# Four transfers instead of five for the last weight matrix of a decode step, and the order of the blocks that use it

## The chip, the cores and the metric

The kernel runs on one core of a Trainium2 chip. Its time is the device time of one execution in microseconds (us). Four executions of the kernel before the change took 84.27 to 84.72 us, with a median of 84.5 us.

## The reference

One decode step of a transformer block with conditioning, for a batch of 4 rows of 512 numbers, in bfloat16. A vector `mod` is computed from the condition `c`; it holds shifts, scales and gates. Then come attention over the last 1024 positions of a cache (32 query heads, 8 key and value heads, 128 numbers a head), and a feed-forward layer:

```python
mod = (silu(c) @ w_mod)                       # sa, ca, ga, sb, cb, gb: 512 each
h = layernorm(x) * (1 + ca) + sa
x = x + ga * attention(h, k_cache, v_cache, wq, wo)
h = layernorm(x) * (1 + cb) + sb
x = x + gb * (relu(h @ w1) @ w2)              # w1 512 x 1792, w2 1792 x 512
```

Some 32 MB of weights and cache are read from memory for 4 rows, so there is little arithmetic for each byte.

## The kernel before

**Transfers.** All large loads are issued by SP on one DMA queue, in the order in which they are needed: `w_mod`, the first two pieces of the key cache, `wq`, the other keys, the values, `wo` in four pieces (lines 120 and 121), `w1` whole (line 126), and `w2` in the pieces that `W2_CHUNKS` lists (lines 128 to 133). A transfer has a semaphore that is counted up when all of it has landed. Eight such semaphores are used in turn, so SP issues a transfer only when the one eight places earlier has landed. `w2` has 1792 rows. They are handled as 14 blocks of 128 rows, and a transfer of `e` blocks puts `e` successive rows of `w2` into each of the 128 partitions, as one run of `e` times 1024 bytes. Within a transfer of `e` blocks, block `m` therefore holds every `e`-th row.

**The feed-forward layer.** The first product must give its results in the same order of rows. So `w1_cols` (line 477) picks 128 columns of `w1` for block `m` with a step of `e` between them. `ffn1` (line 489) computes `relu(h @ w1)` for a range of blocks, transposed: for each block, four weight loads of 128 such columns, one for each quarter of the contraction, with a matmul of 32 columns behind each. Three VectorE operations (lines 498, 500 and 501) then form `uT`. It runs for blocks 0 to 7 and then for blocks 8 to 13.

**The second product.** `closing` (line 192) issues the matmuls of one or more blocks of `w2`. The 512 output columns are cut into four groups of 128. Each block takes two steps `x`, and in each of them two matmuls of 128 columns, `g` = 0 and 1, which use two of TensorE's four groups of 32 array columns side by side. Blocks in `ZUP` (0, 1, 2, 3, 6, 7, 8) add into `za_ps` in column groups 2 and 3; the others (4, 5, 9, 10, 11, 12, 13) add into `z_ps` in column groups 0 and 1. Where `closing` is given one block of each kind, the four matmuls of a step run in all four column groups together; blocks that stand alone use half of the array. TensorE takes its matmuls in the order in which they are written. A block waits for its own transfer and for its part of `uT`.

**The end.** Once block 8, the last of `ZUP`, is added, ScalarE copies `za_ps` to `zc` (line 513), and VectorE multiplies it by the gate and adds the residual (lines 514 and 515). Once block 13 is added, VectorE forms `zg` from `z_ps` (line 520) and adds `zc` to it (line 522). VectorE works in this order, so `zg` stands behind both operations on `zc`. Two small transfers, from SP and from ScalarE's queue, write the result.

The order of the work on TensorE, ScalarE, VectorE and GpSimd is the order in which the program is written.

Of the kernel before, what the change touches and what calls it, by code (L numbers as in the profile page):

```python
# [17 lines left out]
def kernel(  # L18
# [23 lines left out]
    FT = Dff // P  # L42
# [82 lines left out]
    w2_sb = w12[:, DT * Dff:DT * Dff + FT * D].rearrange("p (m n) -> p m n", m=FT)  # L125
    nc.sync.dma_start(out=w1_sb, in_=B_w1.rearrange("(p t) n -> p t n", t=DT))

    W2_CHUNKS = [(0, 4), (4, 4), (8, 3), (11, 2), (13, 1)]
    assert sum(e for _, e in W2_CHUNKS) == FT
    w2_dst = w12[:, DT * Dff:DT * Dff + FT * D]  # L130
    for (m0, e) in W2_CHUNKS:
        nc.sync.dma_start(out=w2_dst[:, m0 * D:(m0 + e) * D],
# [59 lines left out]
    def closing(parts):  # L192
        for x in range(NX):
            for (ps, q, j, src, rhs, start, stop, cols) in parts:
                for g in range(2):
                    q0 = (q + g) * CG
                    nc.tensor.matmul(out=ps[q0:q0 + CG, cols], lhsT=rows(src, j, x), rhs=rhs(2 * x + g),  # L197
                                     start=start and x == 0, stop=stop and x == NX - 1, tile_position=(0, q0))
# [278 lines left out]
    def w1_cols(t, m):  # L477
        m0, e = [ch for ch in W2_CHUNKS if ch[0] <= m][-1]
        return w1_sb[:, t, m0 * P + m - m0:(m0 + e) * P:e]
# [9 lines left out]
    def ffn1(m0, m1):  # L489

        u4_ps = psA.tile([P, m1 - m0, NR, 2, B], f32, tag="t", name=f"u_ps_{m0}")
        u_ps = u4_ps[:, :, 0]
        for m in range(m0, m1):
            for t in range(DT):
                nc.tensor.matmul(out=u4_ps[:, m - m0].rearrange("p n s b -> p n (s b)"), lhsT=w1_cols(t, m),  # L495
                                 rhs=ab[:, t].rearrange("p s b -> p (s b)").unsqueeze(1).to_broadcast([P, NR, 2 * B]), start=(t == 0), stop=(t == DT - 1))
        us = work.tile([P, m1 - m0, B], f32, name=f"us_{m0}")
        nc.vector.tensor_tensor(out=us[:], in0=u_ps[:, :, 0, :], in1=rstd2[:].unsqueeze(1).to_broadcast([P, m1 - m0, B]),
                                op=ALU.mult)
        nc.vector.tensor_tensor(out=us[:], in0=us[:], in1=u_ps[:, :, 1, :], op=ALU.add)  # L500
        nc.vector.tensor_scalar_max(out=put(uT32[:, m0:m1, :]), in0=us[:], scalar1=0.0)  # L501

    def zpart(m):
        mine = ZUP if m in ZUP else ZLOW
        return (za_ps if m in ZUP else z_ps, 2 if m in ZUP else 0, m, uT32, lambda j: w2_sb[:, m, j * DH2:(j + 1) * DH2],
                m == mine[0], m == mine[-1], slice(None))

    for (m0, m1) in [(0, 8), (8, FT)]:
        ffn1(m0, m1)
    for ms in [(0,), (1,), (2, 4), (3, 5), (6,), (7,), (8, 9)]:  # L510
        closing([zpart(m) for m in ms])
    zc = work.tile([2 * CG, DH2], f32, name="zc")
    nc.scalar.copy(out=zc[:], in_=za_ps[2 * CG:P, :])
    nc.vector.tensor_tensor(out=zc[:], in0=zc[:], in1=gb2[:], op=ALU.mult)  # L514
    nc.vector.tensor_tensor(out=zc[:], in0=zc[:], in1=x12_ps[:], op=ALU.add)
    for m in range(10, FT):
        closing([zpart(m)])

    zg = work.tile([2 * CG, DH2], f32, name="zg")
# [36 lines left out]
```

## Time and profile before

| | |
|---|---|
| median of four executions | 84.5 us (84.27 to 84.72) |
| the profiled execution's own time | 84.35 us |
| its span, from the first to the last instruction | 82.6 us |
| mean granted TensorE clock | 0.791 |
| TensorE busy with matmuls, with weight loads | 57.0 us, 46.9 us |
| VectorE, ScalarE, GpSimd busy | 26.5, 23.8, 6.0 us |
| read from memory | 31.99 MB, 387 GB/s over the span |

The span is 1.75 us shorter than the profiled execution's own time; what lies around it is not in the trace. Times within the trace are counted from the start of the span. In a line of the timeline the first number is the start in us and the second how long the group of instructions took, from the start of the first to the end of the last; "x8" is their number; PE is TensorE's matmuls, PEld its weight loads, DVE VectorE, ACT ScalarE and SP the engine that issues the loads. Square brackets hold the idle time of the engine before the group and what ended it. In a table of windows a row holds a stretch of the span, its length, the busy time and number of instructions of PE, PEld, DVE, ACT and POOL, then the granted TensorE clock (1.00 is full), the busy share of the core's 16 DMA engines, and GB/s.

### The profile page before, as it was taken

What the parts mean: (1) busy time and instruction counts of PE and PEld (TensorE: products, weight loads), DVE (VectorE), ACT (ScalarE), POOL (GpSimd) and SP (SyncE); (2) the same over time, 40 slices, a digit from 0 to 9 for tenths busy, and PEclk for the clock granted to TensorE, in tenths of its full rate; (3) what the DMA queues carried; (4) which work ended last, traced back from release to release, by engine and by line L of the source; (5) the groups of instructions that cost most, each with busy time, mean ns of one, the idle gap of its engine ahead of it and who ended that gap; (6) DMA issues with size and microseconds to landing.
All of it is one profiled execution on the core that took longest, in us unless ns stands there. A gap on an engine that the chain in (4) does not pass through costs nothing.

```text
span 82.6 us, 2381 instructions
## 1 busy us (share of the span) xinstructions
PE 57.0 (69%) x1068; PEld 46.9 (57%) x1068; DVE 26.5 (32%) x76; ACT 23.8 (29%) x38; POOL 6.0 (7%) x21
## 2 busy tenths in 40 slices
PE   0001006999962989999999932999837579899950
PEld 0000006995852973997777702999837239577830
DVE  0111300368043010275466576850001320150450
ACT  3201001664302000597779809540100010002010
POOL 5895000000000000000000000000000000000000
PEclk9999999999985555699999999569655555555599
DMA  1999999998979999999999999999999999999700
GB/s 25 325 463 429 393 421 425 571 413 365 492 329 409 441 421 417 429 437 409 421 437 433 417 417 437 417 425 433 433 413 417 437 417 440 432 389 411 304 30 2
DMA packets 4257, 32.14 MB, mean 389 GB/s; under 512 B 528, under 2 KB 664, under 8 KB 1304
## 3 DMA queue, kind: packets, MB, share of 16 engines
q1 hardware_dynamic: 4192, 31.99, 92.6%
q8 instruction: 8, 0.13, 0.6%
q0 software_dynamic: 32, 0.00, 0.0%
q10 hardware_dynamic: 24, 0.01, 0.0%
q14 instruction: 1, 0.01, 0.0%
HBM read 31.99 MB, written 0.00 MB: 387 GB/s over the span
## 4 chain that ended last, share of the span: by engine, by line
DMA 80%; PE 8%; SPq 4%; DVE 3%; issue 1%; ACT 0%; DVEq 0%
DMA k<-in_A_k_cache_dram 33%; DMA v<-in_A_v_cache_dram 24%; DMA wo_sb<-in_A_wo_dram 24%; SPq L86 2%; PE za_ps L197 2%; PE y_ps L440 2%; PE u_ps L495 1%; PE x_ps L197 1%; PE sc_ps L446 1%; SPq L101 1%; PE s_ps L457 1%; SPq L96 0%; SPq L95 0%; DVE zc L514 0%; DVE res L522 0%
## 5 line engine op out<-in xcount | busy, mean ns | idle before, releaser
L228 PE MATMUL ktp<-ident_k,k 128*128 128x128 bf16 x256 | 18.2, 240 | 5.6 <-DMA k<-in_A_k_cache_dram 5.6
L228 PEld LDWEIGHTS <-k 128*128 128x128 bf16 x256 | 17.1, 109 | 8.3 <-DMA k<-in_A_k_cache_dram 5.7
L233 ACT COPY kT<-ktp 128x1024 bf16<-128x1024 bf16 x16 | 15.5, 1015 | 17.4 <-PE ktp L228 16.3
L231 DVE COPY kT<-ktp 128x1024 bf16<-128x1024 bf16 x16 | 11.1, 692 | 16.2 <-PE ktp L228 15.9
L363 PE MATMUL oT_ps<-pT,v 128*128 128x16 bf16 x256 | 7.1, 172 | 1.7 <-issue 1.7
L363 PEld LDWEIGHTS <-v 128*128 128x128 bf16 x256 | 7.0, 100 | 1.7 <-issue 1.7
L240 PE MATMUL sc_ps<-kT,qpad 128*32 128x512 bf16 x64 | 5.6, 445 | 0.4 <-DVE qpad L329 0.4
L380 PE MATMUL pT_ps<-ident_bf,p_rep 128*128 128x128 bf16 x32 | 3.3, 292 | 2.9 <-DVE p_rep L374 2.9
L203 PE MATMUL tp<-ident_bf,cx_sb 8*128 8x8 bf16 x4 | 0.3, 174 | 7.2 <-DMA cx_sb<-in_A_x_dram 7.2
L380 PEld LDWEIGHTS <-p_rep 128*128 128x128 bf16 x32 | 2.9, 135 | 3.4 <-DVE p_rep L374 3.4
L325 PE MATMUL qT_ps<-hT,wq_sb 128*128 128x4 bf16 x128 | 3.6, 166 | 1.4 <-DVE ab L318 1.4
L325 PEld LDWEIGHTS <-wq_sb 128*128 128x128 bf16 x128 | 3.5, 104 | 1.5 <-DMA wq_sb<-in_A_wq_dram 1.5
L203 PEld LDWEIGHTS <-cx_sb 8*128 8x128 bf16 x4 | 0.2, 114 | 7.2 <-DMA cx_sb<-in_A_x_dram 7.2
L432 ACT COPY y<-y_ps 128x256 f32<-128x256 f32 x1 | 0.4, 373 | 9.0 <-DVE y L431 9.0
L440 PEld LDWEIGHTS <-wo_sb 128*128 128x128 bf16 x64 | 2.5, 121 | 0.4 <-DMA wo_sb<-in_A_wo_dram 0.4
L374 DVE TENSOR_TENSOR p_rep<-e_sb,mi 128x512 int32<-128x512 int32 x4 | 2.5, 688 | 0.7 <-ACT e_sb L369 0.7
L440 PE MATMUL y_ps<-o,wo_sb 128*128 128x32 bf16 x64 | 2.5, 193 | 0.3 <-DMA wo_sb<-in_A_wo_dram 0.3
L405 DVE TENSOR_TENSOR oT_sb<-oT_ps,rb 128x128 bf16<-128x128 f32 x1 | 0.3, 291 | 7.5 <-PE oT_ps L363 7.5
L436 PEld LDWEIGHTS y_ps<-sel_b,y 128*128 128x128 f32 x8 | 1.8, 329 | 1.4 <-DVE y L431 1.4
L427 PE MATMUL y_ps<-wo_sb,o 128*32 128x512 bf16 x16 | 1.9, 619 | 0.9 <-DVE o L418 0.9
L240 PEld LDWEIGHTS <-qpad 128*32 128x32 bf16 x64 | 1.3, 103 | 2.2 <-DVE qpad L329 0.7
L197 PEld LDWEIGHTS <-uT 128*32 128x32 bf16 x56 | 2.1, 127 | 0.7 <-DVE uT L501 0.3
(115 smaller groups left out, 57.7 us busy)
## 6 DMA issues: line engine op xcount, KB each, us to landing
k<-in_A_k_cache_dram SPq DMA_DIRECT2D x8, 1024.0 KB, 28.1
v<-in_A_v_cache_dram SPq DMA_DIRECT2D x8, 1024.0 KB, 19.6
wq_sb<-in_A_wq_dram SPq DMA_DIRECT2D x1, 4096.0 KB, 23.5
wo_sb<-in_A_wo_dram SPq DMA_DIRECT2D x4, 1024.0 KB, 19.6
wmod_sb<-in_w_mod_dram SPq DMA_DIRECT2D x1, 2304.0 KB, 9.4
w<-in_B_w_dram SPq DMA_DIRECT2D x1, 1792.0 KB
w<-in_B_w_dram SPq DMA_DIRECT2D x2, 512.0 KB, 19.6
wmod_sb<-in_w_mod_dram SPq DMA_DIRECT2D x1, 768.0 KB, 4.4
```

The lines of the kernel that those rows point to most:

```text
L197: nc.tensor.matmul(out=ps[q0:q0 + CG, cols], lhsT=rows(src, j, x), rhs=rhs(2 * x + g), start=start and x == 0, stop=stop and x == NX - 1, ...
L228: nc.tensor.transpose(out=tp[:, ii, :], in_=k_tiles[gi][:, iq * IQ + ii, :], identity=ident_k)
L231: nc.vector.tensor_copy(out=dst, in_=tp[:])
L233: nc.scalar.copy(out=dst, in_=tp[:])
L240: nc.tensor.matmul(out=sc_ps[hw * CG:(hw + 1) * CG, half * HALF:(half + 1) * HALF], lhsT=qpad[:, b, par, hw, :], rhs=kT[:, half * (NI // 2 ...
L325: nc.tensor.matmul(out=qT_v[:, hq, :], lhsT=wq_sb[:, t, hq * Dh:(hq + 1) * Dh], rhs=hT[:, t, :], start=(t == 0 and hq == 0), stop=(t == DT ...
L363: nc.tensor.matmul(out=oT_ps[:, hw, par].rearrange("p b r -> p (b r)"), lhsT=v_tiles[h][:, i, :], rhs=pT[:, i, c0:c0 + B * rep], start=(fi ...
L374: nc.vector.tensor_tensor(out=p_w[:, ws, :], in0=e_w[:, ws].unsqueeze(2).to_broadcast([P, WQ // 2, B]), in1=mi4[:].unsqueeze(1).to_broadca ...
L380: nc.tensor.transpose(out=tp[:, ii, :], in_=p_rep[:, i // 2, :, i % 2], identity=ident_bf[:])
L427: nc.tensor.matmul(out=y4_ps[q0:q0 + CG, :], lhsT=o4[:, l, g % 2, g // 2, :], rhs=wo_sb[:, g, l, :], start=(g == 0 and l < 4), stop=(g == ...
L436: nc.tensor.matmul(out=y32_ps[:, t, :], lhsT=y4[:, t, :], rhs=sel_b[:], start=(t == 0), stop=False)
L440: nc.tensor.matmul(out=y32_ps[:, m, :], lhsT=wo_sb[:, g, l, m::DT], rhs=o4[:, l, g % 2, g // 2, :], start=False, stop=(g == NP - 1 and l = ...
```

## The change

`w2` is cut into transfers of 6, 5, 2 and 1 blocks in place of 4, 4, 3, 2 and 1. The step between the columns of `w1` follows it through `w1_cols`. In the second product, block 7 is issued together with block 9 and block 8 together with block 10, where block 7 stood alone, blocks 8 and 9 were together and block 10 came alone after the operations on `zc` had been written.

```diff
-    W2_CHUNKS = [(0, 4), (4, 4), (8, 3), (11, 2), (13, 1)]
+    W2_CHUNKS = [(0, 6), (6, 5), (11, 2), (13, 1)]
...
-    for ms in [(0,), (1,), (2, 4), (3, 5), (6,), (7,), (8, 9)]:
+    for ms in [(0,), (1,), (2, 4), (3, 5), (6,), (7, 9), (8, 10)]:
         closing([zpart(m) for m in ms])
     zc = work.tile([2 * CG, DH2], f32, name="zc")
     nc.scalar.copy(out=zc[:], in_=za_ps[2 * CG:P, :])
     nc.vector.tensor_tensor(out=zc[:], in0=zc[:], in1=gb2[:], op=ALU.mult)
     nc.vector.tensor_tensor(out=zc[:], in0=zc[:], in1=x12_ps[:], op=ALU.add)
-    for m in range(10, FT):
+    for m in range(11, FT):
         closing([zpart(m)])
```

## The prediction

> **What bounds the kernel now.** I read the page's slices first, then the chain that ended last, then the issues of the transfers, and then the last six microseconds instruction by instruction, since the change touches nothing earlier. The page's row of DMA shares:
>
> ```profile
> DMA  1999999998979999999999999999999999999700
> ```
>
> The 16 DMA engines are full from the second slice to the thirty-seventh: the kernel is a stream of loads with work hung on it. The chain of waits says the same, and what follows the stream (start, us, what):
>
> ```profile
> 51.13 19.47 DMA wo_sb<-in_A_wo_dram
> ...
> 78.05 0.59 PE za_ps L197 x9
> ...
> 78.78 0.27 ACT zc L513
> ...
> 79.08 0.30 DVE zc L514
> ...
> 79.39 0.28 DVE zc L515
> 79.67 0.26 DVE zg L520
> ```
>
> So the end of the span hangs on the last blocks of `w2`, by way of `za_ps`, its copy and three VectorE operations. When the blocks arrive follows from the issues (w is `w1` and `w2`; KB each, us from issue to landing):
>
> ```profile
> w<-in_B_w_dram SPq DMA_DIRECT2D x2, 512.0 KB, 19.6
> w<-in_B_w_dram SPq DMA_DIRECT2D x1, 384.0 KB, 17.4
> w<-in_B_w_dram SPq DMA_DIRECT2D x1, 256.0 KB, 15.7
> w<-in_B_w_dram SPq DMA_DIRECT2D x1, 128.0 KB, 13.5
> ```
>
> and from SP's timeline, whose last load is this one:
>
> ```profile
> 65.76 0.33 SPq L132 DMA_DIRECT2D w<-in_B_w_dram  x1
> ```
>
> The last transfer lands at 65.76 + 13.5 = 79.26; in the same way (issues at 55.99, 58.43, 60.86 and 63.29; the view of the tile w gives 20.2 for the first, so 19.0 for the second) the others land at 76.19, 77.43, 78.3 and 78.95. TensorE's timeline over the end:
>
> ```profile
> 74.90 1.14 PEld L495 LDWEIGHTS <-w 128*128 128x128 bf16 x32 [0.57 <-DMA w<-in_B_w_dram]
> 75.86 0.83 PEld L495 LDWEIGHTS <-w 128*128 128x128 bf16 x27
> 76.96 0.29 PE L197 MATMUL za_ps<-w,uT 128*32 128x128 bf16 x2 [0.16 <-DVE uT L501]
> 77.78 0.64 PE L197 MATMUL za_ps<-w,uT 128*32 128x128 bf16 x8
> 78.34 0.29 PE L197 MATMUL za_ps<-w,uT 128*32 128x128 bf16 x2
> 78.98 0.62 PE L197 MATMUL z_ps<-w,uT 128*32 128x128 bf16 x12
> ```
>
> The reader sees `ffn1` start when `w1` lands, the second product start at 76.96 when `uT` is made, blocks 6 and 7 (the x8) at 77.78, and then two starts, 78.34 for block 8 and 78.98 for block 11, each just after a landing. The clock over this stretch, from the table of windows:
>
> ```profile
> 77.50:78.75 1.25, 1.25 (x38) 1.16 (x35) 0.00 (x0) 0.00 (x0) 0.00 (x0) 0.50 0.49 185
> 78.75:79.00 0.25, 0.22 (x7) 0.06 (x3) 0.00 (x0) 0.22 (x1) 0.00 (x0) 0.85 0.17 57
> 79.00:79.25 0.25, 0.25 (x8) 0.25 (x8) 0.17 (x1) 0.04 (x1) 0.00 (x0) 1.00 0.00 0
> ```
>
> It goes from half to full at about 78.82 (0.85 is 0.3 of the slice at 0.5 and 0.7 at 1.0). Only half of the DMA engines still work after 77.5: the others are done.
>
> **The change, step by step.**
>
> *One transfer fewer.* The bytes are the same. A straight line through 1.24 us for 4 blocks (76.19 to 77.43), 0.90 for 3 and 0.64 for 2 (TensorE's releases 77.44, 78.34, 78.98) gives 0.30 us a block and 0.03 a transfer, with 0 and 0.12 as the ends that its pairs allow. I take 0.03. The first new transfer (blocks 0 to 5) lands near 76.8, before `uT` needs it. The second (6 to 10) ends where the old third ended, with one transfer fewer ahead of it: block 6 is released at 78.34 - 0.03 = 78.31. Blocks 11 and 12 come at 78.95 and block 13's transfer lands at 79.23. SP issues four times in place of five, 0.33 us each, beside a queue that is full for some 13 us ahead: nothing. No other queue is passed by anything, and the output's transfers only take other semaphores, whose earlier transfers (`wo`) are long landed.
>
> *Blocks 6 and 7 lose their early transfer.* This is the main term. They ran from 77.78, on the second old transfer; now block 6 waits at the head of TensorE's queue until 78.31, and behind it wait 7 to 10, all of the tail, and `zc`. From the release to the end of `za_ps`, the old order had two steps (8 with 9, x = 0 and 1): 78.34 to 78.75 (the copy starts at 78.78, 0.03 after). The new one has six: two of block 6, two of 7 with 9, two of 8 with 10. A step costs 0.107 us: four take 0.64 in the x8 row, of which the last matmul is 0.31. The first interval after a stall is 0.08 to 0.09 (0.40 less that 0.31). So the sixth step starts at 78.31 + 0.08 + 4 x 0.107 = 78.82, just as the clock rises; the last matmul takes 0.22 at full clock (the shortest of `z_ps`, 216 ns), and `za_ps` ends at 79.04 in place of 78.75. The copy moves from 78.78 to 79.07: 0.29 later. Blocks 9 and 10 ride beside and cost no step.
>
> *What the tail gives back.* Block 10 leaves the tail, which holds 11 to 13 alone: they end at about 79.57, against 79.60, so `z_ps` no longer decides. `zg` now started 0.25 after the addition to `zc` (79.39 to 79.64) because `z_ps` was ready only then. Independent VectorE operations follow each other 0.07 before the earlier one's end (72.34 with 0.17, then 72.44), so `zg` can start 0.21 after: 0.04 back. Net: 0.29 - 0.04 = 0.25.
>
> *Wider steps in `w1`.* Blocks 0 to 5 are read with a step of 6 elements and 6 to 10 with 5, where 0 to 7 had 4 and 8 to 10 had 3. The two PEld rows: with step 4 a load costs (1.14 - 0.12) / 31 = 33 ns; the 27 of the second row, three of them still step 4, come to (0.83 - 0.10 - 0.10) / 23 = 27 ns for steps 3, 2 and 1. No row has steps 5 or 6. The low end is 27 (as step 3), the high end twice 33 = 67 (no reason excludes it), and the value I take is in proportion to the step, 8.3 ns an element, since 4 is the nearest row: 42 and 50 ns. Blocks 0 to 7 then take 24 x 17 + 8 x 9 = 480 ns longer, `uT` and block 0 move from 76.96 to 77.44, and block 6's turn comes at 77.78 + 0.48 = 78.26. Its cover is the wait for the transfer until 78.31; 0.05 us of it is left, so on the path it costs nothing. Second half: 480 + 12 x 15 = 660 ns later, its `uT` near 78.1, before block 9's turn at 78.5. At 27 or 33 ns TensorE only idles longer. At 67 ns the 32 loads take 1.09 longer, block 6 comes at 78.87, now at full clock with steps of 0.054: `za_ps` ends at 78.87 + 0.27 + 0.22 = 79.36, 0.61 later, and with the 0.04 back 0.57.
>
> The Trainium skill, "SBUF — State Buffer", in the section on the DMA port swizzle, has 16-byte lines and lets bf16 stride up to 8 elements for free. By it steps of 5 and 6 would cost nothing, and the sum would be 0.25 all the same, with an idle TensorE before block 6. The 33 against 27 ns of steps 4 and 3 here does not agree with it.
>
> *The clock.* The trace shows one execution, with the rise at 78.82. Without a rise, `za_ps` would end at 79.13 and the change would cost 0.34 against this execution. With a full clock from 78.3 on, the six steps take 0.27 + 0.22 and end near 78.8; `zg` is then ready at about the time that `z_ps` gives today, and the cost is about 0.
>
> The same skill, "TensorE: Matmul & The Clock Gate", Part 1, says that the clock follows activity in free-running windows of 3.4 us that do not start with the kernel. By it the rise would fall elsewhere in other executions, and the mean cost would lie between 0 and 0.34; no run here shows this yet.
>
> **Sum.** 0.25 us on 84.35, the profiled execution's own time (82.6 of span and 1.75 around it), gives 84.60. That execution was 0.15 under the median of the four, so against 84.5 I say 84.75, slower by 0.3%. About 0.5%, 0.42 us, is what a measurement of this kernel can tell from no change.
>
> **The rivals.**
> 1. *The wide steps cost more than in proportion,* and `ffn1` in place of the transfer releases block 6. For it: only 0.05 us of cover is left. Against it: steps 1 to 3 cost the same. At 67 ns: 84.5 + 0.57 = 85.07; slower by over 0.42 from about 59 ns on.
> 2. *The delay is covered:* the clock is full by 78.3, or `z_ps` decides the end. For it: both paths met at 79.64 within 0.04. Against it: the clock was half until 78.82 here. Time 84.5.
> 3. *Faster, by the DMA engines that lag:* the table shows half of them idle from 77.5, while the others work on to 78.8, some 1.3 us behind. If larger rows were shared out so that all ended together, each landing would come up to 0.65 us earlier; block 6 would be released near 77.66, TensorE's turn (77.78 or later) would decide, and the end would come some 0.45 earlier: 84.05. It decides from 0.6 us of lag removed. Against it: each transfer still gives every partition one run, as before.
>
> **How the numbers follow.** The forecast 0.50, with its own range 84.5 to 85.0; rival 1 0.30, rival 2 0.12, rival 3 0.08. Slower by over 0.5%: most of rival 1 (0.25) and the forecast's upper edge, 0.34 with a clock that stays half and some 0.1 by which medians scatter (0.18): 0.43. Faster: rival 3, 0.08. Within: 0.49. For 8 in 10 the range goes from 84.4 (rival 2 with the spread of medians) to 85.2 (rival 1 with the same).
>
> **What the changed profile would show.** Step 1: the last `w` transfer lands 0 to 0.1 us earlier against `w1`. Step 2: `za_ps` starts again (block 6) right after the second transfer, near 78.3, and ends near 79.05; the copy at line 513 starts 0.3 us later. Step 3: `zg` follows the addition by 0.21, with TensorE done before it. Step 4: the first 32 loads of line 495 take 1.6 us, and block 0 starts near 77.4. The prediction is wrong if block 6 starts on `uT` and not on a transfer, if loads of step 6 take over 55 ns, or if the landings move by more than 0.1 us.

## The result

The changed kernel takes 84.81 us (median of 30 executions, 84.54 to 85.12) against 84.48 us (49 executions of the kernel before, 84.23 to 85.12). The ratio is 1.0040, with a 95% interval of 1.0031 to 1.0049: 0.33 us slower, small but measured. The forecast was 84.75.

The chain of waits of the changed kernel (start, us, what), span 83.1 us, own time 84.86:

```profile
51.02 19.78 DMA wo_sb<-in_A_wo_dram
...
75.23 2.29 PE u_ps L495 x56
...
79.06 0.21 PE za_ps L197 x4
...
79.29 0.27 ACT zc L513
...
79.59 0.29 DVE zc L514
...
79.90 0.28 DVE zc L515
80.18 0.21 DVE zg L520
...
80.42 0.28 DVE res L522
```

The links are the same as before: the stream of loads, the feed-forward layer, `za_ps`, its copy and VectorE. Two executions differ in when the stream arrives, so I count from the first weight load of line 495, which starts when `w1` lands: 74.90 before, 75.09 here. Counted so, the copy at line 513 starts 3.88 us after `w1` before and 4.20 now (0.32 later), and the last addition (line 522) 5.06 before and 5.33 now (0.27 later). That addition is this line of the chain before:

```profile
79.96 0.28 DVE res L522
```

So in these two executions the loss lies between the landing of `w1` and the copy of `za_ps`.

The transfers of `w2` (KB each, us to landing), and the issue of two of them by SP:

```profile
w<-in_B_w_dram SPq DMA_DIRECT2D x1, 768.0 KB, 20.9
w<-in_B_w_dram SPq DMA_DIRECT2D x1, 640.0 KB, 20.0
w<-in_B_w_dram SPq DMA_DIRECT2D x1, 256.0 KB, 18.2
w<-in_B_w_dram SPq DMA_DIRECT2D x1, 128.0 KB, 16.1
```

```profile
58.42 0.33 SPq L132 DMA_DIRECT2D w<-in_B_w_dram  x1
63.28 0.33 SPq L132 DMA_DIRECT2D w<-in_B_w_dram  x1
```

The second transfer lands at 58.42 + 20.0 = 78.4, the last at 63.28 + 16.1 = 79.4. TensorE and VectorE over the same stretch; the lines are taken from several short windows of the timeline, so a group ends where its window does, and lines between them are left out:

```profile
75.09 1.20 PEld L495 LDWEIGHTS <-w 128*128 128x128 bf16 x24 [0.55 <-DMA w<-in_B_w_dram]
76.23 0.85 PEld L495 LDWEIGHTS <-w 128*128 128x128 bf16 x19
77.52 0.40 PE L197 MATMUL za_ps<-w,uT 128*32 128x128 bf16 x4
77.61 0.29 PE L197 MATMUL z_ps<-w,uT 128*32 128x128 bf16 x2
77.92 0.32 PE L197 MATMUL za_ps<-w,uT 128*32 128x128 bf16 x2
78.14 0.59 PE L197 MATMUL za_ps<-w,uT 128*32 128x128 bf16 x6
78.81 0.45 PE L197 MATMUL za_ps<-w,uT 128*32 128x128 bf16 x4
80.11 0.28 DVE L520 TENSOR_TENSOR zg<-z_ps,gb 64x128 f32<-64x128 f32 x1
```

The six matmuls from 78.14 are the two steps of block 3 and then block 6's first, which ends at 78.73; a matmul after a stall takes 0.29, so block 6 begins near 78.44 (the trace's own record of it starts at 78.43), just after the landing. The last of `za_ps` ends at 78.81 + 0.45 = 79.26. The clock, from the table of windows, stays half to the end here:

```profile
78.50:79.00 0.50, 0.50 (x22) 0.49 (x20) 0.00 (x0) 0.00 (x0) 0.00 (x0) 0.50 0.31 107
79.00:79.50 0.50, 0.50 (x18) 0.45 (x11) 0.00 (x0) 0.21 (x1) 0.00 (x0) 0.50 0.00 0
```

In the kernel before it was half up to 78.82, past the start of the copy at 78.78, so the 0.32 us at the copy is no effect of the clock.

### The profile page after: what moved, and what is told of

It reads as the page before. It is cut to its first block, busy times and chain, and to the rows that moved or that the text cites. A ratio compares the mean times of both kernels' runs of the same rounds, so it can differ in the third digit from the quotient of the medians.

```text
span 83.1 us, 2380 instructions
## 1 busy us (share of the span) xinstructions
PE 57.1 (69%) x1068; PEld 47.1 (57%) x1068; DVE 26.5 (32%) x76; ACT 23.8 (29%) x38; POOL 6.0 (7%) x21
## 4 chain that ended last, share of the span: by engine, by line
DMA 80%; PE 9%; SPq 4%; DVE 2%; issue 1%; ACT 0%
DMA k<-in_A_k_cache_dram 33%; DMA wo_sb<-in_A_wo_dram 24%; DMA v<-in_A_v_cache_dram 24%; PE u_ps L495 3%; SPq L86 2%; PE za_ps L197 2%; PE y_ps L440 2%; PE x_ps L197 1%; PE sc_ps L446 1%; PE s_ps L457 1%; SPq L101 1%; SPq L96 0%; SPq L95 0%; DVE zc L514 0%; DVE res L522 0%
## 5 line engine op out<-in xcount | busy, mean ns | idle before, releaser
L233 ACT COPY kT<-ktp 128x1024 bf16<-128x1024 bf16 x16 | 15.5, 1015 | 17.1 <-PE ktp L228 16.1
L495 PEld LDWEIGHTS <-w 128*128 128x128 bf16 x56 | 2.3, 131 | 0.6 <-DMA w<-in_B_w_dram 0.6
```

What stands on the lines that cost most here:

```text
L233: nc.scalar.copy(out=dst, in_=tp[:])
```

## The experiments

The theory: blocks 6 and 7 now arrive with 8 to 10, so six steps into `za_ps` stand behind a landing where two did, and the wider steps in `w1` are covered by the wait for that landing. The rivals: the wider steps set the end, or the new pairing of blocks costs something itself.

The table gathers the profiles, all in us after the first weight load of line 495. "Block 0" is the first matmul of the second product, "copy" is line 513, "last add" the start of line 522. "Clock" is where it last became full in that execution, in us of its span ("half": not again before the end). Each kernel was profiled once for each row. In the rebalanced kernel's profile those loads waited for an earlier operation and not for `w1`, so its columns are left out.

| kernel | transfers, order | ratio, 95% interval | block 0 | copy | last add | clock |
|---|---|---|---|---|---|---|
| before | 4 4 3 2 1, old | 1 | 2.06 | 3.88 | 5.06 | 78.8 |
| the change | 6 5 2 1, new | 1.0040 (1.0031 to 1.0049) | 2.43 | 4.20 | 5.33 | half |
| the change again | 6 5 2 1, new | 1.0051 (1.0032 to 1.0070) | 2.43 | 4.25 | 5.38 | 79.8 |
| transfers only | 6 5 2 1, old | 1.0047 (1.0030 to 1.0065) | 2.43 | 4.31 | 5.43 | 79.9 |
| order only | 4 4 3 2 1, new | 1.0005 (0.9992 to 1.0018) | 2.06 | 3.78 | 5.01 | 77.6 |
| step 3 | 6 5 2 1, new | 1.0025 (1.0008 to 1.0042) | 1.96 | 4.26 | 5.38 | half |
| step 3 again | 6 5 2 1, new | 1.0036 (1.0018 to 1.0054) | 1.98 | 3.98 | 5.10 | 77.8 |
| 6 and 7 cut off | 6 2 3 2 1, new | 1.0014 (1.0001 to 1.0026) | 2.33 | 4.05 | 5.18 | 79.3 |
| the same, step 3 | 6 2 3 2 1, new | 1.0002 (0.9984 to 1.0019) | 1.93 | 3.88 | 5.01 | 78.6 |
| longer wait | 6 7 1, new | 1.0118 (1.0096 to 1.0140) | 2.83 | 4.90 | 6.03 | half |
| rebalanced | 6 5 2 1, block 8 for 4 | 1.0022 (1.0000 to 1.0044) | - | - | - | 77.1 |
| tail of ones | 4 4 3 1 1 1, old | 1.0031 (1.0012 to 1.0050) | 2.06 | 3.68 | 5.05 | 78.9 |
| tail of ones again | 4 4 3 1 1 1, old | 1.0036 (1.0021 to 1.0051) | 2.06 | 3.68 | 5.00 | 77.4 |

### The two halves of the change by themselves

Transfers only:

```diff
-    W2_CHUNKS = [(0, 4), (4, 4), (8, 3), (11, 2), (13, 1)]
+    W2_CHUNKS = [(0, 6), (6, 5), (11, 2), (13, 1)]
```

> The four new transfers with the old order of blocks. Theory (blocks 6 and 7 wait for the second transfer, so that six steps into za_ps follow its landing in place of two): the order matters little, so the whole loss is here: 0.33 us slower than before, 84.8 us, ratio 1.004, block 6 released near 78.4 and za_ps ended near 79.25. Rival (the new pairing of blocks costs): as before, 84.5 us, ratio 1.000.

Order only:

```diff
-    for ms in [(0,), (1,), (2, 4), (3, 5), (6,), (7,), (8, 9)]:
+    for ms in [(0,), (1,), (2, 4), (3, 5), (6,), (7, 9), (8, 10)]:
...
-    for m in range(10, FT):
+    for m in range(11, FT):
```

> The five old transfers with the new pairs 7 with 9 and 8 with 10. Theory: the second step of block 7 now stands behind block 9, which waits for the third transfer, so three steps into za_ps follow that landing in place of two: 0.107 us less the 0.04 that the tail gives back, some 0.05 to 0.1 slower, ratio 1.0006 to 1.0012. Rival (the pairing costs): 0.33 us slower, ratio 1.004.

Measured: 84.85 against 84.44 us (1.0047) for the transfers, 84.56 against 84.44 (1.0005) for the order. The transfers carry the loss. The pairing by itself shows none; its interval leaves room for 0.15 us. The profile of the transfers alone shows why the pairing could not help there either; TensorE's timeline:

```profile
78.19 0.69 PE L197 MATMUL za_ps<-w,uT 128*32 128x128 bf16 x6
78.58 0.29 PE L197 MATMUL z_ps<-w,uT 128*32 128x128 bf16 x2
78.66 0.34 PE L197 MATMUL za_ps<-w,uT 128*32 128x128 bf16 x2
```

The `z_ps` matmuls at 78.58 are block 9, written behind the first step of block 8; they start before block 7 does (78.66). Once the transfer had landed, the two pairs of column groups each went on at their own pace, so what was written as 8 with 9 ran beside 6 and 7 anyway.

### The wider steps in w1

The first transfer's rows are laid out as two runs of three blocks, so that blocks 0 to 5 read `w1` with a step of 3; the number of transfers and their blocks stay.

```diff
-    W2_CHUNKS = [(0, 6), (6, 5), (11, 2), (13, 1)]
+    W2_LOADS = [(0, 6), (6, 5), (11, 2), (13, 1)]
+    W2_CHUNKS = [(0, 3), (3, 3), (6, 5), (11, 2), (13, 1)]
...
-    for (m0, e) in W2_CHUNKS:
-        nc.sync.dma_start(out=w2_dst[:, m0 * D:(m0 + e) * D],
-                          in_=B_w2[m0 * P:(m0 + e) * P, :].rearrange("(q e) n -> q (e n)", e=e))
+    for (m0, e) in W2_LOADS:
+        s = min(e, 3) if e == 6 else e
+        nc.sync.dma_start(out=w2_dst[:, m0 * D:(m0 + e) * D].rearrange("q (j n) -> q j n", j=e // s),
+                          in_=B_w2[m0 * P:(m0 + e) * P, :].rearrange("(j q e) n -> q j (e n)", j=e // s, e=s))
```

> The change, with the rows of the first transfer laid out as two runs of three per partition, so that blocks 0 to 5 read w1 with a step of 3 in place of 6; still four transfers. The first 32 weight loads then take 24 x 27 + 8 x 40 ns = 0.97 us in place of 1.44. Theory: uT comes 0.47 us earlier, TensorE waits for the second transfer instead, and the end stays: 84.8 us, ratio 1.004 (up to 0.07 more, since the 128 rows of 6 KB become 256 of 3 KB). Rival (the wide steps are the loss): 84.4 to 84.5 us, ratio 0.999 to 1.000.

Measured: 84.68 against 84.44 us, 1.0025. That lies between the theory and the rival, but the timeline is plain:

```profile
75.02 1.84 PEld L497 LDWEIGHTS <-w 128*128 128x128 bf16 x56 [0.65 <-DMA w<-in_B_w_dram]
78.42 0.29 PE L199 MATMUL za_ps<-w,uT 128*32 128x128 bf16 x2 [0.40 <-DMA w<-in_B_w_dram]
79.28 0.26 ACT L515 COPY zc<-za_ps 64x128 f32<-64x128 f32 x1 [4.28 <-PE za_ps L199]
```

The 56 loads take 1.84 us where the changed kernel's take 2.31 (2.29 in the chain above), and block 0 starts 0.47 earlier. All of it is then spent idle: TensorE waits 0.40 us for the second transfer, block 6 starts at 78.42 as ever, and the copy comes 4.26 after `w1` (4.20 in the change). To settle the time, the change and this kernel were run again side by side.

> The change itself once more, beside the next kernel on the same chip. Theory: ratio 1.003 to 1.005 against the kernel before.

> The change with steps of 3 for blocks 0 to 5, once more, now on the same chip as the change: the first comparison (1.0025 against 1.0040, on different chips) left open whether the wide steps take a third of the loss. Theory (they are covered by the wait for the second transfer): within 0.1 us of the change. Rival (they cost a part): 0.1 to 0.15 us faster than the change.

Measured: 84.92 us for the change, 84.89 with step 3, 0.03 apart, against 84.51 before. The intervals alone would still allow 0.1, and on the first chip the transfers alone, with the steps of 6, had taken 84.85 where this kernel took 84.68. So the times don't settle it. The idle time does: in both profiles with step 3 TensorE sits idle before block 6 (0.40 and 0.45 us), so an earlier `uT` starts it no earlier.

### Blocks 6 and 7 in a transfer of their own

```diff
-    W2_CHUNKS = [(0, 6), (6, 5), (11, 2), (13, 1)]
+    W2_CHUNKS = [(0, 6), (6, 2), (8, 3), (11, 2), (13, 1)]
```

> The change, with the second transfer cut into 6 and 7, and 8 to 10 (6, 2, 3, 2, 1 blocks). Theory: blocks 6 and 7 land near 77.4 and no longer wait; what is left is uT later by 24 x 13 - 8 x 7 ns = 0.27 us, so block 8 has its turn near 78.5 where the transfer would allow 78.34: some 0.1 to 0.15 slower than before, 84.6 us, ratio 1.001 to 1.002, with no wait for a transfer before block 8. Rival (the late release isn't the cause): as the change, 84.8 us, ratio 1.004.

With the first transfer's rows in runs of three as well:

> As the kernel with blocks 6 and 7 cut off (6, 2, 3, 2, 1 blocks), and the first transfer's rows as two runs of three, so that w1 is read with steps of 3, 2, 3, 2 and 1 alone. Theory: both causes are gone, block 8 waits for its transfer as before, and only the new pairs are left: 84.4 to 84.55 us, ratio 0.999 to 1.001; the distance to the kernel with step 6 is what the wide step costs once its cover is gone, 0.05 to 0.15 us. Rival (the pairing or larger transfers cost by themselves): 84.8 us, ratio 1.004.

Measured: 84.59 against 84.44 us (1.0014), and 84.59 against 84.60 on another chip (1.0002). Letting 6 and 7 land early takes away most of the loss. That the rest goes with the wide step is what the medians say, but their intervals overlap; the profiles show how. TensorE and ScalarE in the first of the two, whose third transfer lands at 78.3:

```profile
77.29 0.40 PE L197 MATMUL za_ps<-w,uT 128*32 128x128 bf16 x4 [0.17 <-DVE uT L501]
77.80 0.85 PE L197 MATMUL za_ps<-w,uT 128*32 128x128 bf16 x12
78.65 0.32 PE L197 MATMUL za_ps<-w,uT 128*32 128x128 bf16 x2
79.01 0.26 ACT L513 COPY zc<-za_ps 64x128 f32<-64x128 f32 x1 [4.04 <-PE za_ps L197]
```

`za_ps` is added from 77.29 to its last step at 78.65 without a gap: here `uT`, late by the steps of 6, sets the end, not a landing. With steps of 3:

```profile
76.94 0.40 PE L199 MATMUL za_ps<-w,uT 128*32 128x128 bf16 x4 [0.24 <-DVE us L500]
78.39 0.29 PE L199 MATMUL z_ps<-w,uT 128*32 128x128 bf16 x2
78.40 0.29 PE L199 MATMUL za_ps<-w,uT 128*32 128x128 bf16 x2
78.89 0.26 ACT L515 COPY zc<-za_ps 64x128 f32<-64x128 f32 x1 [3.95 <-PE za_ps L199]
```

TensorE waits for the third transfer again: block 9 starts at 78.39, and the step into `za_ps` at 78.40 is the second of block 7, which is written behind block 9 and stands idle with it. Three steps follow this landing, as the order of the change has it, where the kernel before had two. The copy is back at 3.88 us after `w1`. In this execution the clock was full from 78.6, which shortened the last step; but the kernel before has the same 3.88 at half clock. So the wide step costs about 0.17 us at the copy once its cover is gone, and nothing while it has it.

### The wait made longer

```diff
-    W2_CHUNKS = [(0, 6), (6, 5), (11, 2), (13, 1)]
+    W2_CHUNKS = [(0, 6), (6, 7), (13, 1)]
```

> The suspected wait made longer: transfers of 6, 7 and 1 blocks, order as in the change, so that blocks 6 to 12 all wait for one transfer that lands two blocks (0.6 us) later. Theory: za_ps ends 0.6 us later than in the change: 85.4 us, ratio 1.010 to 1.012. Rival (wide steps set the start of the second product and so the end): step 7 for 8 of the first 32 loads adds 0.1 us to the change: 84.9 us, ratio 1.005.

Measured: 85.61 against 84.60 us, 1.0118, where the theory had 1.010 to 1.012. TensorE and ScalarE:

```profile
75.17 2.80 PEld L495 LDWEIGHTS <-w 128*128 128x128 bf16 x56 [0.57 <-DMA w<-in_B_w_dram]
76.32 1.54 PEld L495 LDWEIGHTS <-w 128*128 128x128 bf16 x27
79.21 0.29 PE L197 MATMUL za_ps<-w,uT 128*32 128x128 bf16 x2 [0.17 <-DMA w<-in_B_w_dram]
80.07 0.26 ACT L513 COPY zc<-za_ps 64x128 f32<-64x128 f32 x1 [4.84 <-PE za_ps L197]
```

Block 6 waits for the larger transfer, even though step 7 makes the first product later still, and the copy follows 0.86 us after its start (0.85 in the changed kernel): the same six steps behind a landing 0.7 us later.

### Fewer steps behind the landing

```diff
-    ZUP = (0, 1, 2, 3, 6, 7, 8)
+    ZUP = (0, 1, 2, 3, 4, 6, 7)
...
-    for ms in [(0,), (1,), (2, 4), (3, 5), (6,), (7, 9), (8, 10)]:
+    for ms in [(0,), (1,), (2, 5), (3,), (4,), (6, 8), (7, 9)]:
...
-    for m in range(11, FT):
+    for m in range(10, FT):
```

> The change with block 4 added into za_ps and block 8 into z_ps, so that four steps into za_ps follow the second landing in place of six. Theory: za_ps ends 0.2 us earlier than in the change; z_ps then has 12 steps after the landing and comes near to deciding: 0.1 to 0.2 us faster than the change, 84.65 us, ratio 1.001 to 1.003. Rival (not the steps behind the landing): as the change, ratio 1.004.

Measured: 84.82 against 84.60 us, 1.0022 (1.0000 to 1.0044). The direction is the expected one, but the interval holds the ratio of the change too, so the time alone proves nothing. Its executions spread the widest (84.33 to 85.26); the profiled one had a full clock from 77.1 and cannot be set beside the half-clock profile of the change. This experiment leaves the price of a step open; the 0.82 us that six steps take is read from the profiles.

### A finer tail for the kernel before

```diff
-    W2_CHUNKS = [(0, 4), (4, 4), (8, 3), (11, 2), (13, 1)]
+    W2_CHUNKS = [(0, 4), (4, 4), (8, 3), (11, 1), (12, 1), (13, 1)]
```

> The kernel before with its fourth transfer of two blocks cut into two of one (4, 4, 3, 1, 1, 1). Theory: block 11 lands 0.3 us earlier and is done before 12 lands, so that in executions with half the clock at the end two steps less stand behind the last landings: 0 to 0.1 us faster, 84.4 us, ratio 0.999 to 1.000. Rival (a transfer more costs some 0.1 us): 84.6 us, ratio 1.001.

> Six transfers (4, 4, 3, 1, 1, 1) once more, on another chip. If a sixth transfer slows the stream of loads by itself: 0.2 to 0.3 us slower than before, ratio 1.003. If the first result was the spread of that chip: ratio 0.999 to 1.001.

Measured: 84.86 against 84.60 us (1.0031), and on another chip 84.88 against 84.51 (1.0036). It was expected to be faster than the kernel before, and it is slower by as much as the change. It isn't the chip. In the two profiles, counted from `w1`, nothing is lost: the last add comes at 5.05 and 5.00 against 5.06. But the loads of line 495 start at 75.53 and 75.52, later than in any of the other profiles (74.86 to 75.26). The two lines, one from each profile:

```profile
75.53 1.78 PEld L495 LDWEIGHTS <-w 128*128 128x128 bf16 x56 [0.57 <-DMA w<-in_B_w_dram]
75.52 1.80 PEld L495 LDWEIGHTS <-w 128*128 128x128 bf16 x56 [0.52 <-DMA w<-in_B_w_dram]
```

So in these executions the time is lost in the stream of loads before `w1` has landed, although the transfers that differ are queued behind it. The traces, which hold the landing of every DMA engine's part of a transfer, say where: from the third piece of `wo` on, which lands at 68.8, one of the 16 engines lands its parts 0.42 to 0.61 us after the other 15, while in the other eleven profiles the last engine is at most 0.22 behind. The sixth transfer is issued only at 68.81. Both executions were also among the slowest of their kernel (85.18 and 85.15 us), so they show more than the medians lost. Why that engine falls behind, and whether the sixth transfer has to do with it, stays open.

## Why the prediction was right

*One transfer fewer: 0.03, between 0 and 0.12.* Counted from `w1`, the block after the second landing started 3.35 us later here against 3.44 for the third landing before (78.34 less 74.90); in the profile of the transfers alone it was again 3.44. So 0 to 0.1, and no more can be told.

*Blocks 6 and 7, the main term: 0.29 at the copy.* The copy came 0.32 later. The six steps took 0.82 us from block 6 to the end of `za_ps` (78.44 to 79.26). The prediction had 0.73 with the clock rising at the last step and 0.82 without a rise; without one is what this execution shows. The landing was some 0.07 us earlier against `w1` than predicted, which nearly makes up for the 0.09: that the copy came so close to 0.29 is in part luck.

*The tail gives back 0.04.* `zg` started 0.21 after the addition (79.90 to 80.11), as said, against 0.25.

*Wider steps: no cost on the path.* The loads took (1.20 - 0.15) / 23 = 46 ns at step 6 and (0.85 - 0.13) / 18 = 40 at step 5, against the 50 and 42 assumed. Block 3 took its last step one before block 6, at 78.24, so block 6's turn would have come at 78.35; the landing held it until 78.43. The cover left was 0.08, where the prediction had 0.05. Rival 1, which lived on that margin, fell with the 46 ns. The kernel with blocks 6 and 7 cut off shows `ffn1` deciding once the landing comes early enough, but at 46 ns a load it costs 0.17 us at the copy, where rival 1 had 0.61 at 67 ns.

*The clock: between about 0 and 0.34.* The profiles hold both ends. With half clock throughout, the last add was 0.27 later than before (0.34, less a landing some 0.1 earlier where 0.03 was assumed). The kernel with step 3 had, in its second profile, a full clock while block 6 waited, here in the windows:

```profile
77.50:78.00 0.50, 0.50 (x18) 0.38 (x9) 0.15 (x1) 0.00 (x0) 0.00 (x0) 0.66 0.63 231
78.00:78.50 0.50, 0.05 (x6) 0.03 (x5) 0.00 (x0) 0.00 (x0) 0.00 (x0) 1.00 0.44 170
78.50:79.00 0.50, 0.48 (x20) 0.31 (x20) 0.00 (x0) 0.00 (x0) 0.00 (x0) 1.00 0.31 109
```

and its last add came at 5.10, only 0.04 after the kernel before. So rival 2 can come near to true in a single execution (shown on the kernel with step 3; no profile of the change has an early rise), and the median does not follow it. Nor does the clock make the loss: of the change's 30 executions, the 13 with a mean clock under 0.77 took 84.81 us in the median and the 15 with 0.79 to 0.80 took 84.85, while the kernel before, measured again on three chips, took 84.31 to 84.62 in every such group. In every profile the clock changes at whole multiples of 3.41 us from its first change, and its last rise falls anywhere from 77.1 to 79.9, or not at all. The Trainium skill, "TensorE: Matmul & The Clock Gate", Part 1, has the clock follow free-running windows of activity; these times fit that.

*Rival 3* did not come true: half of the DMA engines still stand idle over the last stretch (0.46 and 0.50 busy from 77.5 to 78.5 in the changed kernel).

The sum, 0.25, came out as 0.27 in the profiles and 0.33 in the medians. What the prediction took for granted, as the description of the kernel does, and the runs contradict is that TensorE keeps the written order of all its matmuls: in the changed kernel block 4 (the `z_ps` line at 77.61) starts before the first step of block 2 (77.92), behind which it is written. It did not matter because the path goes through `za_ps`, whose own order holds, and a wait for a transfer does hold back what is written behind it: in the kernel with 6 2 3 2 1 and step 3, block 7's own transfer had landed at 77.4, and its second step still stood until 78.40, behind block 9.

## What to carry to other kernels

Work that uses a transfer waits for all of it, so when transfers are merged, look for the work that used to run while the rest of the larger one was still on its way: its price is the time of the serial steps that now stand behind the landing, and it can be read from the timeline before. A cost that hides under a wait comes out when the wait goes; here the wide step was free in the change and cost about 0.17 us as soon as the wait was taken away. Saving a transfer in this queue, which is always full, saved 0.1 us at most.

## What the runs showed of the hardware

- **Weight loads by step.** From one load of 128 bf16 columns to the next it took 27 ns at steps 1 to 3, 33 at 4, 40 at 5, 46 at 6 and 53 at 7 ((1.54 - 0.15) / 26 in the profile with transfers of 6, 7 and 1), all at half clock: some 6.7 ns for each element beyond 3. A matmul of 32 columns follows each load, so the 27 ns may be the matmul's and not the load's. The Trainium skill, "SBUF — State Buffer", in the section on the port swizzle, lets bf16 stride up to 8 elements for free; for weight loads these runs differ.
- **Column groups at their own pace.** Matmuls written behind others in another pair of column groups started up to 0.3 us ahead of them (77.61 against 77.92). A wait for a transfer held both pairs (block 7's second step at 78.40, behind block 9 at 78.39, in the kernel with 6 2 3 2 1 and step 3).
- **A sixth small transfer** went with 0.26 and 0.37 us more on two chips, and in both profiles with one DMA engine 0.4 to 0.6 us behind the rest before `w1` landed. No run tells why.
- **Half of the DMA engines lag.** In the kernel before, after each load of instructions one more of the 16 engines lands its part of every later transfer late: some 1.8 us after the first engine, where the rest take about 0.3 in the median. Seven such loads of 16 KB start at 23.4, 32.4, 40.2, 48.3, 58.8, 64.7 and 71.3 us and one of 8 KB at 67.0. One engine is late in the transfer that starts to land at 24.6, three at 44.2, five at 63.8, eight at 74.2. A transfer is released with its last part (in the changed kernel the second one's lands at 78.39, and block 6 starts at 78.43), so these engines set the releases at the end. No run tested that the instruction loads cause it.
